# Row maxima 20 steps ahead of the exponentials instead of 22, and a head's row of maxima issued with its last maximum

## The chip, the cores and the metric

The kernel runs on one core of a Trainium2 chip. The metric is the device time of one execution in microseconds (us), lower is better; a time is the median of several runs. Engines are named as the profile names them: PE is the matrix engine (PEld its weight loads), DVE the vector engine, ACT the scalar engine, POOL the GpSimd engine, SP the engine that issues most DMAs.

## What is computed

Two attentions over the same 2048 rows of width 576, 32 heads of width 18 each, are mixed by a gate. A has keys and values per head, B shares one key and one value head among its 32 query heads.

```
x = A_x                                     # 1 x 2048 x 576, float32
g = sigmoid((x * gate_w).sum(-1, keepdims=True))
a = concat_heads(softmax(q_h k_h^T * 18**-0.5) v_h) @ wo       # 32 heads, qkv = x @ A_wqkv
b = concat_heads(softmax(q_h k^T  * 18**-0.5) v) @ wo          # 32 heads, one k and one v
out = g * a + (1 - g) * b
```

All products are made of float32 numbers cut into a high and a low part, so a head's queries and keys take 54 rows (18 times three products) of the 128 partitions, and 54 and 56 rows fit into each half. TensorE can then work on the two halves of its rows at once: rows 64 to 119 for one matmul (`MB`), rows 0 to 55 for another (`SB`).

## The kernel before, in words

The program is one long order written by hand. The 64 heads (0 to 31 of B, 32 to 63 of A) run one after the other. A head has 16 **steps**; step T (0 to 1023, head T // 16) is 128 keys against all 2048 queries: four score matmuls of 512 queries (`step_scores`, L742), four exponentials on ACT (L750), and the products with the values, summed in one PSUM bank `acc` (`step_pv`, L757).

Softmax needs the maximum of each query's scores before its exponentials. So the same scores are also made the other way round, 128 queries against 512 keys at a time, and reduced along the keys (`step_max`, L697). Block M of 128 queries (head M // 16) has 2048 keys, four pieces of 512. A piece is one matmul and one DVE reduction (the letter `m`, L706). Two pieces can also be made by one reduction: ACT takes the relu of the difference of the two (`x`, L700), and DVE adds it to the second piece and reduces (`y`, L703). In the main loop two blocks make one pair: one x, one y, six m. The maxima run `LEAD` steps ahead of the exponentials.

When a head's 16 blocks are reduced, `max_rows` makes the **row of maxima**: DVE reduces the four pieces (L713, tile `m`), transposes (L715, tile `mt`), POOL cuts the result into two parts (L240 and L242, tile `mh`; DVE does it for head 1), SP writes it to DRAM (`m_d`) and, when that has landed, reads it back as two more rows of the head's queries (`qs<-m_d`). The score matmuls of the head multiply these rows by ones, and so the exponent is already reduced by the maximum. The first score matmul of a head therefore waits for the last of these DMAs.

Order around the change:

- The **lead** (`lead_steps`) comes before the main loop. Its string interleaves half matmuls of eight projection units (`A` and `B`, two row halves, L965) with x and y for the first maxima; there every two pieces are one x (L1116) and one y (L1122), so a block has two of each. Two last pieces are plain `m`. The row of head 0 is issued by `lead_max` behind the 32nd y. Eight scores (`s`) end the string: steps 0 and 1.
- The **main loop** takes patterns of 8 steps from T = 2 on: `s` is a score, a digit is that many quarter products with the values, `A`, `B` and `U` are pieces of other projections. `TWO14` (six times from T = 10), `HALF14` (to T = 730), `TWO12` (738 to 802), `HALF12` (802 to 930), `DENSE` (946 to 1002), and `PLAIN` at T = 2, 218, 730, 930 and 938.
- The **tail** is a string of its own, with scores and exponentials only. There the scores of a step alternate between the two row halves (`alone`).
- At each even T `begin(T)` issues the loads that are due and one piece of a slow side job (`slow`: normalising finished heads, on SP, POOL and DVE).
- PSUM has seven banks for all of this. A planner (`Clock`) walks along with a model of the engines and gives each matmul the bank that it expects to be free first. It sets no order.

Before, `max_rows` of a head stood at the start of the pattern in which (T + 22) % 16 = 0, so at T % 16 = 10, six steps before that head's exponentials:

```
        if (T + LEAD) % 16 == 0 and (T + LEAD) // 16 - 1 < NU:
            max_rows((T + LEAD) // 16 - 1, nc.gpsimd if T > 16 else nc.vector)
```

Of the kernel before, what the change touches and what calls it, by code (L numbers as in the profile page):

```python
# [21 lines left out]
NU = 2 * H  # L22
# [2 lines left out]
MT = 14  # L25
ROW_KB, ROW_G, ROW_VB, ROW_Q = 0, 18, 32, 50
SCALE = DH ** -0.5
LEAD = 22
NT = 5
FIRST = ((0, 1), (1, 1), (2, 1), (0, 2), (0, 3), (1, 2), (2, 2), (1, 3), (2, 3))  # L30
PRODS = (("h", "h"), ("h", "l"), ("l", "h"))
# [125 lines left out]
def gated_mix_kernel(ctx: ExitStack, tc: tile.TileContext, xT, wall, wv, wo, out):  # L157
    nc = tc.nc
# [871 lines left out]
    NSTEP = 16 * NU  # L1030
# [31 lines left out]
    slow = [gates()]  # L1062
# [21 lines left out]
                             start=True, stop=True, skip_group_check=True)  # L1084

    pos = {"s": 0, "P": 0, "x": (LEAD + 2) // 2, "y": (LEAD + 2) // 2}
    pairs = {"x": [(M, h) for M0 in range(0, LEAD + 2, 8) for h in range(2) for M in range(M0, M0 + 8)][:-1]}
    pairs["y"] = list(pairs["x"])

    def lead_units():  # L1090
# [36 lines left out]
    def lead_steps(ops):  # L1127

        for op in ops.replace(" ", ""):
# [12 lines left out]
            else:  # L1142
# [5 lines left out]
    lead_steps("AABABABABABxBAABxyABxBAyABxyABxBAyABxyABABxyABABxyABABABxyAB"  # L1148
               "ABxyABABxyABABxyABABxyABABxyABABYBABxBABABxyABABxyABABxyABAB"
               "xyABABxyABABYBABxBAABxyABABxyAgBABxyABABxyABABxyABABYBABxBAA"  # L1150
               "BxyABABxyABABxyABABxyABABxyABABYBABxBAABxyABABxyAgBABxyABABx"
               "yABABxyABABABxyABABxyABABxyAgBABxyABABxyABABxyABAsABxyABABxs"
               "AyABxyABBYsBBBsBB"
               "ssmsms")
    clk.half = HALF_MM

    PLAIN = "mssmsm 4 smsmsm 3 smmssx 3 smmsys 3 mssxysm 3 msxmssm 3 mssysms 3 msssmys 4 msmsms 3 smxssm 3"
# [8 lines left out]
    def begin(T):  # L1166

        for f in at.get(T, []) + at.get(T + 1, []):
            f()
        if slow and T % 16 != 10:  # L1170
            for _ in range(2 if T > 1000 or 914 < T < 930 else 1):
                if slow:
                    try:
                        next(slow[0])
                    except StopIteration:
                        slow.pop(0)

    out_last = out_proj(8, [P])

    def emit(ops, units=0):  # L1180
        for op in ops.replace(" ", ""):
            if op == "s":
                if pos["s"] % 8 == 0:
                    begin(pos["s"] // 4)
                step_scores(*bank(pos["s"]), pos["s"] // 4 >= NSTEP - LEAD, pos["s"] % 4)
                pos["s"] += 1
            elif op == "f":
                keep_busy()
            elif op in "xy":

                if (op == "x" or pos["x"] == pos["y"]) and 2 * pos["x"] < NSTEP:
                    step_max(*divmod(2 * pos["x"], 16), "x")
                    pos["x"] += 1
                if op == "y":
                    step_max(*divmod(2 * pos["y"], 16), 0)
                    pos["y"] += 1
            elif op == "m":
                M, c = plain.pop(0)
                step_max(*divmod(M, 16), c)
            elif op in "AB":  # L1200
                if units:
                    half_step(op.lower())
            elif op == "U":
                u = next_unit() if units else None
                if u:
                    whole_unit(u)
                    units -= 1
            elif op == "V":
                whole_unit(next(out_last))
            elif op in "abc":  # L1210
                if op == "a":
                    while slow:
                        run(slow.pop(0))
                    L["half"] = last_sums(pos["P"] // (4 * NSTEP))
                next(L["half"])
                if op == "a" and not pos["P"] // (4 * NSTEP):
                    next(out_last)
            else:
                n = 1 if op == "P" else int(op)
                while n:  # L1220
                    last, h = divmod(pos["P"], 4 * NSTEP - 64)
                    if last:
                        k = min(n, 2 - h % 2)
                        last_pv(h // 32, h % 32 // 2, 128 * (h % 2), 128 * (h % 2 + k))
                    else:
                        T, a = divmod(pos["P"], 4)
                        k = min(n, 4 - a)
                        step_pv(*divmod(T, 16), 128 * a, 128 * (a + k))
                    pos["P"] += k
                    n -= k  # L1230
                    if pos["P"] % 64 == 0 and pos["P"] < 4 * NSTEP:
                        head_out(pos["P"] // 64 - 1)
# [1 line left out]
    open_ph2()  # L1234
    begin(0)
    emit("x")
    while pos["s"] < 4 * (NSTEP - LEAD):
        T = pos["s"] // 4
        if (T + LEAD) % 16 == 0 and (T + LEAD) // 16 - 1 < NU:
            max_rows((T + LEAD) // 16 - 1, nc.gpsimd if T > 16 else nc.vector)  # L1240
        if T >= SEG[1][3] + 4:
            emit(DENSE, 4)
        elif T in TWICE:
            emit(TWO14, 2)
        elif VB <= T < RB - 8 or RB <= T < RE:
            emit(HALF14, 1)
        elif RE + 8 <= T < RE + 8 * 9:
            emit(TWO12, 2)
        elif RE + 8 * 9 <= T < RE + 8 * 25:
            emit(HALF12, 1)  # L1250
        else:
            emit(PLAIN)
    max_rows(NU - 1)


    emit("ssssss 8 ssssssUssss 7 ssssss 8 ssssss 9 ssssssUssss 7 ssssss 9 ssssssUsssss 7 ssss 6 ssssss 3 a 6 ssssssbUcssss 6 ssssssVVVVVVVVsssssss 9 9 2", 4)
    assert pos["s"] == pos["P"] == 4 * NSTEP
    emit("a V b V V c")
    for u in out_last:
# [35 lines left out]
```

## Time and profile before

| what | value |
|---|---|
| time, median of 3 runs | 2633.17 us (2632.41 to 2634.5) |
| profiled execution: span from first to last instruction | 2632.7 us |
| busy: PE, PEld, DVE, ACT, POOL | 99%, 53%, 91%, 93%, 33% of the span |
| TensorE clock granted | 1.000 |

The page gives the profiled execution as its span alone; no time of its own is shown beside it, and the median of the runs stands 0.4 us above the span. A row of a timeline reads: start and duration in us, engine, line, operation, output<-input, shapes, how many, and in brackets how long the engine sat idle before it and what released it. PE's busy time is modelled to the end of each pipelined matmul, so 99% does not say that it runs at its peak. In the rows, `mx<-bank` is a reduction to maxima, `pt<-bank` an exponential, `bank<-qs,ksb` (L742) a score, `bank<-ksb,qs` (L697) a matmul for a maximum.

### The profile page before, as it was taken

To read this page: it belongs to the slowest core of one execution; us is meant where nothing else is said; L and a number is where in the kernel's file an instruction comes from. 1 tells how busy PE (TensorE), PEld (TensorE's weight loads), DVE (VectorE), ACT (ScalarE), POOL (GpSimd) and SP (SyncE) were. 2 spreads that over 40 slices of the span, in tenths; PEclk is the share of its full clock that TensorE was granted. 3 is DMA by queue.
4 is the path that set the end of the run, shared out by engine and by line. 5 is a ranking of instruction groups with operands and counts; after the bars stand their busy time and mean duration, and the time that the engine had idled before them with its cause. 6 is when DMAs were issued, how large, how long until landed. Compare 5 with 4: busy or idle time off the path is not lost.

```text
span 2632.7 us, 66902 instructions
## 1 busy us (share of the span) xinstructions
PE 2619.6 (99%) x25197; PEld 1402.5 (53%) x25197; DVE 2395.2 (91%) x4575; ACT 2446.7 (93%) x4862; POOL 860.7 (33%) x1108
## 2 busy tenths in 40 slices
PE   9999999999999999999999999999999999999999
PEld 7655545545555455454554555545555544545665
DVE  6899999999999999999999999999998999999883
ACT  5999999999999999999999999999999999999887
POOL 5611000211365535643554446443310020012113
PEclk9999999999999999999999999999999999999999
DMA  8412111212343234323544344434422332233312
GB/s 255 141 58 61 36 48 56 74 52 72 97 117 112 88 98 116 116 90 93 149 133 138 119 130 148 143 116 123 141 95 76 100 97 85 63 88 123 112 56 93
DMA packets 176520, 270.43 MB, mean 103 GB/s; under 512 B 59161, under 2 KB 137705, under 8 KB 164817
## 3 DMA queue, kind: packets, MB, share of 16 engines
q1 hardware_dynamic: 159125, 211.39, 28.1%
q0 software_dynamic: 16032, 53.25, 5.5%
q8 instruction: 198, 3.24, 0.5%
q10 hardware_dynamic: 1040, 1.52, 0.2%
q14 instruction: 125, 1.02, 0.1%
HBM read 190.26 MB, written 66.90 MB: 98 GB/s over the span
## 4 chain that ended last, share of the span: by engine, by line
PE 96%; DMA 1%; POOL 1%; SPq 1%; issue 0%; ACT 0%; DVE 0%; ACTq 0%; POOLq 0%
PE acc L757 39%; PE bank L697 29%; PE bank L742 17%; PE bank L965 10%; SPq L163 1%; PE acc L769 1%; PE bank L945 1%; DMA xsh<-xT 0%; PE bank L278 0%; DMA ksb<-kq 0%; DMA ke<-pdhl 0%; POOL oacc L938 0%; POOL phl L242 0%; POOL pst L1099 0%; POOL qk L163 0%
## 5 line engine op out<-in xcount | busy, mean ns | idle before, releaser
L750 ACT ACTIVATE pt<-bank 128x512 f32<-128x512 f32 x4096 | 2145.0, 616 | 122.8 <-PE bank L742 71.3
L706 DVE TENSOR_REDUCE mx<-bank 128x1 f32<-128x512 f32 x3002 | 1885.7, 683 | 118.6 <-PE bank L742 58.1
L742 PE MATMUL bank<-qs,ksb 56*128 56x512 f32 x2688 | 906.9, 424 | 1.5 <-DMA qs<-m_d 1.5
L697 PE MATMUL bank<-ksb,qs 54*128 54x512 f32 x2270 | 806.4, 426 | 0.0
L757 PE MATMUL acc<-pt,vb 128*19 128x256 f32 (+3 forms) x6144 | 553.1, 455 | 0.0
L697 PEld LDWEIGHTS bank<-ksb,qs 54*128 54x128 f32 x2270 | 382.8, 184 | 319.8 <-ACT pt L750 191.2
L757 PE MATMUL acc<-pt,vg 128*19 128x512 f32 (+3 forms) x5952 | 535.1, 455 | 0.0
L742 PEld LDWEIGHTS bank<-qs,ksb 56*128 56x128 f32 x2688 | 441.0, 184 | 156.2 <-DVE mx L706 63.9
L742 PE MATMUL bank<-qs,ksa 56*128 56x512 f32 x1408 | 466.7, 425 | 0.0
L697 PE MATMUL bank<-ksa,qs 54*128 54x512 f32 x1232 | 438.6, 426 | 0.0
L703 DVE CUSTOM_DVE_ANT_0 junk<-bank,xb 128x512 bf16<-128x512 f32 x500 | 342.5, 685 | 29.6 <-PE bank L742 24.3
L700 ACT ACTIVATE xb<-bank 128x512 f32<-128x512 f32 x500 | 292.3, 606 | 13.8 <-PE bank L742 3.0
L697 PEld LDWEIGHTS bank<-ksa,qs 54*128 54x128 f32 x1232 | 207.8, 184 | 150.5 <-ACT pt L750 86.6
L240 POOL CAST mh<-mt 128x32 fp32r<-128x32 f32 x63 | 13.2, 210 | 827.4 <-DVE mt L715 605.3
L742 PEld LDWEIGHTS bank<-qs,ksa 56*128 56x128 f32 x1408 | 225.5, 184 | 84.2 <-DVE mx L706 31.3
L757 PEld LDWEIGHTS acc<-pt,vb 128*19 128x19 f32 x6144 | 123.1, 97 | 203.0 <-issue 169.5
L757 PEld LDWEIGHTS acc<-pt,vg 128*19 128x19 f32 x5952 | 119.7, 97 | 206.9 <-issue 180.9
L240 POOL CAST rhl<-rst 128x292 fp32r<-128x292 f32 (+2 forms) x81 | 34.0, 420 | 486.4 <-issue 304.7
L965 PE MATMUL bank<-xr,wrh 64*128 64x292 f32 (+1 forms) x1134 | 168.2, 300 | 0.0
L697 PE MATMUL bank<-kdb,qs 54*128 54x512 f32 x372 | 159.8, 429 | 0.0
L965 PEld LDWEIGHTS bank<-xr,wrh 64*128 64x128 f32 x1134 | 139.5, 186 | 2.8
L560 POOL TENSOR_TENSOR xr<-xst,xr 128x876 fp32r<-128x876 f32 (+1 forms) x63 | 130.5, 2071 | 0.0
(173 smaller groups left out, 2403.4 us busy)
## 6 DMA issues: line engine op xcount, KB each, us to landing
qs<-qk SPq DMA_DIRECT2D x366, 144.0 KB
xst<-xT SPq DMA_DIRECT2D x54, 438.0 KB
ksa<-qk SPq DMA_DIRECT2D x132, 144.0 KB
qk<-rhl POOLq DMA_DIRECT2D x54, 292.0 KB, 4.3
ksb<-qk SPq DMA_DIRECT2D x60, 144.0 KB
qk<-phl POOLq DMA_DIRECT2D x16, 512.0 KB, 5.7
onh<-oh POOLq DMA_DIRECT2D x32, 256.0 KB, 4.4
onl<-ol POOLq DMA_DIRECT2D x32, 256.0 KB, 4.8
```

The costliest lines, as they stand in the source:

```text
L163: return (eng or nc.sync).dma_start(o, i)
L240: eng_h.tensor_copy(h, src)
L560: nc.gpsimd.tensor_tensor(x[:, 5:8, 0:n], t0, x[:, 0:3, 0:n].bitcast(F32), op=OP.subtract)
L697: nc.tensor.matmul(pm, qs[u % 3][b:b + 54, i * P:(i + 1) * P], k, start=True, stop=True)
L700: nc.scalar.activation(MX["x", u, i], pm, AF.Relu)
L703: nc.vector.tensor_tensor_reduce(junk, pm, MX.pop(("x", u, i)), 1.0, -3e38, op0=OP.add, op1=OP.max, accum_out=MX[u][:, i, c:c + 1])
L706: nc.vector.tensor_reduce(MX[u][:, i, c:c + 1], pm, axis=AX.X, op=OP.max)
L742: nc.tensor.matmul(ps, kst(u)[b:b + 56, i * P:(i + 1) * P], qs[u % 3][b:b + 56, c * 512:(c + 1) * 512], start=True, stop=True)
L750: nc.scalar.activation(pt, ps, AF.Exp, scale=SCALE)
L757: nc.tensor.matmul(acc[32 * j:32 * j + 19, a:b], v_of(u, i), PT[u, i, j][:, a:b], start=(i == 0), stop=(i == 15), skip_group_check=True)
L769: nc.tensor.matmul(acc[32 * j:32 * j + 19, 256 * half + a:256 * half + b], v_of(NU - 1, i), pt[:, x + a:x + b], start=(i == 0), stop=(i == ...
L965: nc.tensor.matmul(u.fp[op][:, 0:u.n], x[b:b + 64], y[b:b + 64], start=(n == 0), stop=(n == last))
```

## The change

`LEAD` goes from 22 to 20. The lead forms 22 blocks of maxima instead of 24: four times `xy` (eight matmuls) are taken out of its string, one of them ahead of the row of head 0, three behind it, and nothing else in it moves. The main loop begins two blocks earlier in the list of maxima, so the tail loses two steps without maxima and gets one more pair in its place (six m and one y; its x stands in the loop). The rows of maxima are no longer issued at a pattern's start but by `formed`, right behind the seventh reduction of a head's last pair; where that is depends on the pattern's string: 1.75 steps into `HALF14`, 2.25 into `TWO14`, 2 into `TWO12`, 2.75 into `PLAIN`, 3 into `HALF12` and `DENSE`. The side job now pauses at T % 16 = 12 and runs at 10.

```diff
-LEAD = 22
+LEAD = 20
...
-    pairs = {"x": [(M, h) for M0 in range(0, LEAD + 2, 8) for h in range(2) for M in range(M0, M0 + 8)][:-1]}
+    pairs = {"x": [(M, h) for M0 in range(0, LEAD + 2, 8) for h in range(2) for M in range(M0, min(M0 + 8, LEAD + 2))][:-1]}
...
-        if slow and T % 16 != 10:
+        if slow and T % 16 != 12:
...
+    FORMED = {}
+
+    def formed(p):
+
+        FORMED[p] = FORMED.get(p, 0) + 1
+        if FORMED[p] == 7 and p % 8 == 7:
+            max_rows(p // 8, nc.gpsimd if p > 15 else nc.vector)
...
                 if op == "y":
                     step_max(*divmod(2 * pos["y"], 16), 0)
                     pos["y"] += 1
+                    formed(pos["y"] - 1)
             elif op == "m":
                 M, c = plain.pop(0)
                 step_max(*divmod(M, 16), c)
+                formed(M // 2)
...
-    while pos["s"] < 4 * (NSTEP - LEAD):
+    while pos["s"] < 4 * (NSTEP - LEAD - 2):
         T = pos["s"] // 4
-        if (T + LEAD) % 16 == 0 and (T + LEAD) // 16 - 1 < NU:
-            max_rows((T + LEAD) // 16 - 1, nc.gpsimd if T > 16 else nc.vector)
...
-    max_rows(NU - 1)
...
-    emit("ssssss 8 ssssssUssss 7 ssssss 8 ...", 4)
+    emit("msmssm 4 smsmsmsys 4")
+    emit("ssssssUss 7 ssssss 8 ...", 4)
```

In the lead the change is seen on DVE around the row of head 0 (`m_610`, `mt`). A row `L1122 ISA junk,mx<-bank,xd` is a y; `L477` is a piece of the side job. Before:

```order
L1122 ISA junk_1060,mx_600<-bank_1058,xd 128x512
L1122 ISA mx_600 128x1
L1122 ISA junk_1072,mx_600<-bank_1070,xd 128x512
L1122 ISA mx_600 128x1
L1122 ISA junk_1080,mx_600<-bank_1078,xd 128x512
L1122 ISA mx_600 128x1
L713 TENSOR_REDUCE m_610<-mx_600 128x16
L715 STREAM_TRANSPOSE mt<-m_610 128x32
L1122 ISA junk_1108,mx_601<-bank_1106,xd 128x512
```

and now, at the same place:

```order
L1122 ISA junk_1064,mx_600<-bank_1062,xd 128x512
L1122 ISA mx_600 128x1
L1122 ISA junk_1072,mx_600<-bank_1070,xd 128x512
L1122 ISA mx_600 128x1
L1122 ISA junk_1091,mx_600<-bank_1089,xd 128x512
L1122 ISA mx_600 128x1
L713 TENSOR_REDUCE m_610<-mx_600 128x16
L715 STREAM_TRANSPOSE mt<-m_610 128x32
L1122 ISA junk_1112,mx_601<-bank_1110,xd 128x512
```

The row stands behind the same 32nd y. What moved is that y itself: with one `xy` gone ahead of it, it stands eight places later in the string (place 219 counted from 0, not 211), and the piece of the side job follows one y behind the row, not two. On POOL the four rows around the row of head 0 stand as they did, the DMA of a projection unit directly ahead of it, before and now alike:

```order
L242 TENSOR_TENSOR phl<-pst,phl 128x512
L163 DMA qk<-phl 128x2x512
L240 CAST mh<-mt 128x32
L242 TENSOR_TENSOR mh<-mt,mh 128x32
L1099 TENSOR_TENSOR pst<-pst,pst_1031 128x512
```

Nothing moved there. In a `HALF14` pattern, head 13, DVE before: `mx_603` holds head 13's maxima, `mx_604` head 14's, and `L703 ISA junk,mx<-bank,xb` is a y.

```order
L706 TENSOR_REDUCE mx_603<-bank_9793 128x1
L713 TENSOR_REDUCE m_611<-mx_603 128x16
L715 STREAM_TRANSPOSE mt<-m_611 128x32
L703 ISA junk,mx_604<-bank_9809,xb 128x512
L703 ISA mx_604 128x1
L706 TENSOR_REDUCE mx_604<-bank_9817 128x1
L706 TENSOR_REDUCE mx_604<-bank_9828 128x1
L706 TENSOR_REDUCE mx_604<-bank_9835 128x1
L706 TENSOR_REDUCE mx_604<-bank_9846 128x1
L706 TENSOR_REDUCE mx_604<-bank_9853 128x1
L706 TENSOR_REDUCE mx_604<-bank_9864 128x1
L706 TENSOR_REDUCE mx_604<-bank_9871 128x1
```

and now:

```order
L703 ISA junk,mx_603<-bank_9768,xb 128x512
L703 ISA mx_603 128x1
L706 TENSOR_REDUCE mx_603<-bank_9776 128x1
L706 TENSOR_REDUCE mx_603<-bank_9787 128x1
L706 TENSOR_REDUCE mx_603<-bank_9794 128x1
L706 TENSOR_REDUCE mx_603<-bank_9805 128x1
L706 TENSOR_REDUCE mx_603<-bank_9812 128x1
L706 TENSOR_REDUCE mx_603<-bank_9823 128x1
L713 TENSOR_REDUCE m_611<-mx_603 128x16
L715 STREAM_TRANSPOSE mt<-m_611 128x32
L706 TENSOR_REDUCE mx_604<-bank_9839 128x1
L706 TENSOR_REDUCE mx_604<-bank_9846 128x1
```

The two rows L713 and L715 have moved from ahead of the pattern's first y to behind that y and six reductions. At the beginning of the tail, DVE before (L940 adds a projection into the output, L781 is the copy of `acc` at the end of a head):

```order
L706 TENSOR_REDUCE mx_602<-bank_44542 128x1
L706 TENSOR_REDUCE mx_602<-bank_44559 128x1
L940 TENSOR_TENSOR oacc<-bank_44509,oacc 128x288
L713 TENSOR_REDUCE m_611<-mx_602 128x16
L715 STREAM_TRANSPOSE mt<-m_611 128x32
L940 TENSOR_TENSOR oacc<-bank_44640,oacc 128x288
L781 COPY oe<-acc 128x512
```

and now:

```order
L940 TENSOR_TENSOR oacc<-bank_44477,oacc 128x288
L706 TENSOR_REDUCE mx_602<-bank_44545 128x1
L706 TENSOR_REDUCE mx_602<-bank_44552 128x1
L706 TENSOR_REDUCE mx_602<-bank_44563 128x1
L706 TENSOR_REDUCE mx_602<-bank_44574 128x1
L706 TENSOR_REDUCE mx_602<-bank_44581 128x1
L706 TENSOR_REDUCE mx_602<-bank_44588 128x1
L703 ISA junk,mx_602<-bank_44595,xb 128x512
L703 ISA mx_602 128x1
L713 TENSOR_REDUCE m_611<-mx_602 128x16
L715 STREAM_TRANSPOSE mt<-m_611 128x32
L940 TENSOR_TENSOR oacc<-bank_44642,oacc 128x288
```

Seven reductions, those of the last pair, have moved from the lead's side of the list into the tail, ahead of the row of head 63.

More of the change, by code (lines that the diff above doesn't have):

```diff
@@ L1150, in gated_mix_kernel @@
                "xyABABxyABABYBABxBAABxyABABxyAgBABxyABABxyABABxyABABYBABxBAA"
[L1151 to L1154, printed above, removed]
+               "BxyABABxyABABxyABABABABxyABABYBABxBAABxyABABxyAgBABABABxyABA"
+               "BxyABABABABABxyABABxyAgBABABABxyABABxyABAsABxyABABxsAyABxyAB"
+               "BYsBBBsBBssmsms")
     clk.half = HALF_MM
@@ L1252, in gated_mix_kernel @@
             emit(PLAIN)
-    max_rows(NU - 1)
-    emit("ssssss 8 ssssssUssss 7 ssssss 8 ssssss 9 ssssssUssss 7 ssssss 9 ssssssUsssss 7 ssss 6 ssssss 3 a 6 ssssssbUcssss 6 ssssssVVVVVVVVsssssss 9 9 2", 4)
+    emit("msmssm 4 smsmsmsys 4")
+    emit("ssssssUss 7 ssssss 8 ssssss 9 ssssssUssss 7 ssssss 9 ssssssUsssss 7 ssss 6 ssssss 3 a 6 ssssssbUcssss 6 ssssssVVVVVVVVsssssss 9 9 2", 4)
     assert pos["s"] == pos["P"] == 4 * NSTEP
```

## The prediction

> **What bounds the kernel now.** I read the page's busy shares first, then the rate of the exponentials stage by stage, then the timeline around the first exponential, around a row of maxima, and at the start of the tail.
>
> ```profile
> span 2632.7 us, 66902 instructions
> PE 2619.6 (99%) x25197; PEld 1402.5 (53%) x25197; DVE 2395.2 (91%) x4575; ACT 2446.7 (93%) x4862; POOL 860.7 (33%) x1108
> ```
>
> PE, DVE and ACT are all above 90%, so no share says which of them sets the pace. The table of stretches, restricted to the exponentials (L750), gives the pace: busy time, count, clock.
>
> ```profile
> 627.90:646.70 18.80, 16.69 (x33) 1.00 0.37 101
> 2116.00:2300.00 184.00, 159.33 (x306) 1.00 0.28 84
> 2441.00:2556.00 115.00, 86.45 (x160) 1.00 0.28 85
> 2567.00:2586.00 19.00, 19.00 (x39) 1.00 0.07 16
> ```
>
> One exponential takes 0.570 us in `PLAIN` (18.80/33), 0.601 in `HALF12`, 0.719 in `DENSE`, and 0.487 in the tail, where ACT is busy without a gap. So ACT sets the pace only in the tail. In the main loop it is the common order of PE, DVE and ACT with seven banks between them. Which engine waits there is seen in one `HALF14` pattern (590 to 609 us, the waits):
>
> ```profile
> PEld bank L697 <- ACT pt L750: 2.7, 4, 0.8
> PEld bank L697 <- DVE mx L706: 0.8, 2, 0.4
> ```
>
> PE waits for banks of ACT more than for banks of DVE, and part of these waits lies under matmuls that still run.
>
> **The lead: four xy removed.** Stretches with all engines (PE, PEld, DVE, ACT, POOL), and then the rows around the row of head 0:
>
> ```profile
> 80.00:85.00 5.00, 5.00 (x44) 3.94 (x42) 4.68 (x16) 4.51 (x9) 4.47 (x7) 1.00 0.53 184
> 85.00:90.00 5.00, 3.53 (x31) 2.62 (x29) 2.79 (x9) 3.46 (x8) 4.38 (x5) 1.00 0.33 111
> ...
> 79.24 0.22 DVE L713 TENSOR_REDUCE m<-mx 128x16 f32<-128x64 f32 x1
> 79.49 0.21 DVE L715 STREAM_TRANSPOSE mt<-m 128x32 f32<-128x32 f32 x1
> ...
> 81.04 0.73 POOL L163 DMA_DIRECT2D qk<-phl  x1 [0.30 <-POOL phl L242]
> 81.77 0.22 POOL L240 CAST mh<-mt 128x32 fp32r<-128x32 f32 x1
> ...
> 82.35 0.34 SPq L163 DMA_DIRECT2D m_d<-mh  x1
> 85.27 1.25 SPq L163 DMA_DIRECT2D qs<-m_d  x2
> ...
> 88.73 0.49 PE L742 MATMUL bank<-qs,ksb 56*128 56x512 f32 x1 [1.47 <-DMA qs<-m_d]
> 89.26 0.60 ACT L750 ACTIVATE pt<-bank 128x512 f32<-128x512 f32 x1 [1.54 <-PE bank L742]
> ```
>
> Until 85 us PE issues 44 matmuls in 5 us, so eight matmuls less are 0.91 us of PE's time; that is what the shorter string is worth at most while PE paces. But the string doesn't set when the exponentials begin. PE reached the first score 1.47 us before its rows of maxima had landed. Follow the chain back: the read was issued at 85.27 because the write `m_d` had to land first, the write stood behind POOL's `mh` at 81.77, and POOL took `mh` only then because it was still busy with a projection unit: its DMA issue of 81.04 ends at 81.77 with no gap, 2.07 us after DVE had `mt` (79.70). That unit's last B stands ahead of the first xy removed, and the order of POOL is unchanged. The 32nd y now comes eight places later in the string, 8 x 5/44 = 0.91 us, so `mt` is there at about 80.6, still 1.2 us before POOL asks for it. Hence `mh`, the write, the read and the first score stay at 81.77, 82.35, 85.27 and 88.73; PE is at the first score 0.91 us earlier and idles 2.4 us instead of 1.47. Behind the first score nothing is removed. I take 0 for the lead. Ends: SP waited for 64 writes of `m_d` 87.6 us in all, 1.37 each,
>
> ```profile
> SPq L163 <- DMA m_d<-mh: 87.6, 64, 2.8
> ```
>
> and this one took 2.58 (82.69 to 85.27), so the chain may be 1.2 us shorter by luck; longer than 2.8 none was. So -1.2 to +0.2. The four relu and four y that go with the eight matmuls are covered by the same idle time.
>
> **The main loop: the row of maxima later in a pattern.** Two questions: does it disturb DVE at its new place, and does it still land in time. DVE in the half of `HALF14` with the row, then in the half without (there the copy of `acc` stands at the same place):
>
> ```profile
> 589.12 0.22 DVE L713 TENSOR_REDUCE m<-mx 128x16 f32<-128x64 f32 x1
> 589.77 0.69 DVE L703 CUSTOM_DVE_ANT_0 junk<-bank,xb 128x512 bf16<-128x512 f32 x1
> 590.39 6.08 DVE L706 TENSOR_REDUCE mx<-bank 128x1 f32<-128x512 f32 x10
> 596.85 0.69 DVE L706 TENSOR_REDUCE mx<-bank 128x1 f32<-128x512 f32 x1 [0.39 <-PE bank L742]
> ...
> 609.29 0.68 DVE L703 CUSTOM_DVE_ANT_0 junk<-bank,xb 128x512 bf16<-128x512 f32 x1
> 609.89 6.06 DVE L706 TENSOR_REDUCE mx<-bank 128x1 f32<-128x512 f32 x10
> 616.27 0.69 DVE L706 TENSOR_REDUCE mx<-bank 128x1 f32<-128x512 f32 x1 [0.31 <-PE bank L742]
> ```
>
> The row costs DVE 0.65 us (589.12 to 589.77). Then come ten reductions without a gap, then 0.39 us in which DVE waits for PE: there the delay has been absorbed. In the changed `HALF14` (heads 4 to 13 and 15 to 45, 41 in all) the row stands behind the sixth of these reductions, so still ahead of that idle time: the end of the run stays where it is. 0. Ends: the two halves run 19.52 us (589.77 to 609.29) and, from head to head at 38.83, 19.31; half of that difference, 0.1 us a head, is 4 us either way. In `HALF12` (heads 51 to 58) the row comes later, behind one idle time of DVE and ahead of others:
>
> ```profile
> 2115.22 0.22 DVE L713 TENSOR_REDUCE m<-mx 128x16 f32<-128x64 f32 x1
> 2121.11 1.29 DVE L706 TENSOR_REDUCE mx<-bank 128x1 f32<-128x512 f32 x2 [0.25 <-PE bank L742]
> 2122.92 0.08 DVE L703 DVE_READ_ACCUMULATOR2_ANT mx<- 128x1 f32 x1
> 2126.78 4.96 DVE L706 TENSOR_REDUCE mx<-bank 128x1 f32<-128x512 f32 x8 [0.25 <-PE bank L742]
> 2133.30 0.69 DVE L706 TENSOR_REDUCE mx<-bank 128x1 f32<-128x512 f32 x1 [0.35 <-PE bank L742]
> ...
> 2116.39 0.36 SPq L163 DMA_DIRECT2D m_d<-mh  x1
> 2117.87 1.24 SPq L163 DMA_DIRECT2D qs<-m_d  x2
> ...
> 2129.58 0.50 PE L742 MATMUL bank<-qs,ksb 56*128 56x512 f32 x1
> ```
>
> It will stand behind 2122.92; the two idle times that follow, 0.25 and 0.35, take 0.60 of its 0.65. Until then DVE gives back banks up to 0.4 us later: 0 to 0.4 us for each of eight heads, 0 to 3; the bank waits above are mostly ACT's, so I take 0.
>
> In time: from the row's start to the end of the second read's issue it is 3.89 us (2115.22 to 2119.11). The landing is bounded by a head whose row was late, head 31: POOL had been held up, and
>
> ```profile
> 1297.60 0.22 POOL L240 CAST mh<-mt 128x32 fp32r<-128x32 f32 x1
> 1300.39 1.25 SPq L163 DMA_DIRECT2D qs<-m_d  x2
> 1303.39 0.39 PE L742 MATMUL bank<-qs,ksb 56*128 56x512 f32 x1
> ```
>
> its first score stood at 1303.39 without a wait, so reads land within 1.75 us of the end of their issue. A round trip is at most 5.64 us. In `HALF12`, the shortest lead with `DENSE` at three steps, the changed row starts at 2123.00 of this time scale and the score stands at 2129.58: 6.58 us, 0.94 to spare. `HALF14` has 1.25 steps more, `DENSE` longer steps. In head 31 POOL's delay lasts past the new start of the row (about 1293.5), so its `mh` stays at 1297.60 and its score in time. No head waits: 0.
>
> The Trainium skill weighs against this: "DMA: Bandwidth & Descriptors", section "Anatomy of one DMA", puts a fixed cost of about 2.0 us on each DMA, nearly all of it the receipt of the write (for DMAs that GpSimd issues). With two of them in a row the round trip would be an estimated 1.17 + 2.0 + 1.24 + 2.0 = 6.4 us, and the spare time 0.2 instead of 0.9. By that rule too no head waits, but little would be needed. The write above was waited for 1.48 us from issue to issue, so this trace is below the rule.
>
> **The tail: two steps get maxima.** Steps 1002 and 1003 had scores alone, 8 x 0.487 = 3.90 us. Now they carry six m and one y. By the `PLAIN` rate they take 8 x 0.570 = 4.56; by `DENSE` 5.75, but no projection is among them; DVE alone needs 7 x 0.606 = 4.24 (6.06 for ten). I take `PLAIN`, +0.7, with ends +0.3 and +1.9. One x more in the last `DENSE` pattern hides, ACT being busy 86.45 of 115 there. The row of head 63 follows:
>
> ```profile
> 2566.38 0.21 DVE L713 TENSOR_REDUCE m<-mx 128x16 f32<-128x64 f32 x1
> 2569.74 2.51 SPq L163 DMA_DIRECT2D qs<-m_d  x4
> 2576.92 1.03 PE L742 MATMUL bank<-qs,ksa 56*128 56x512 f32 x6
> ```
>
> It begins seven reductions later, 2570.6, has two of its four reads issued 4.61 us after that and all four after 5.87, and needs up to 1.75 more: 2577.0 and 2578.2. The head's first score stood at about 2577.2 and moves with the 0.7 to 2577.9, the second, from the other half, right behind. Just in time; 0 to 0.5 us of waiting, I take 0.1.
>
> **Sum:** 0 + 0 + 0.7 + 0.1 = +0.8 us on the span of 2632.7, so 2633.5; the median of the runs stands 0.4 above that span, 2634.0.
>
> **Rivals.** (1) Rows too late, slower. Place: heads 51 to 58, from a round trip over 6.58 us; each microsecond beyond costs eight. A write of 2.8 us, the longest, instead of 1.48 gives 6.96 and 3 us in all. The side job now runs at T % 16 = 10 ahead of `mh` on POOL; with its cast, subtraction and wait in the way another 0.5 us or more is thinkable, some 0.9 us a head, 2641. For: the spare time is short. Against: that job starts three steps before the row. (2) Relief in the main loop, faster: with 0.65 us gone from ahead of the run of ten, PE gets its first banks sooner, and 0.2 us in each of 41 heads stay: -8, 2625. For: DVE runs without a gap there. Against: PE waits for ACT more. (3) The 0.91 us of the lead do arrive, because the write of `m_d` lands sooner: 2633.1. Against: nothing ahead of it on POOL or in the queue has changed.
>
> **How the numbers follow.** My forecast has 0.70 and by its terms' ends 2631.5 to 2638; rival 1 has 0.10, rival 2 0.08, rival 3 0.12. A change below 0.2% (5.3 us) can hardly be told from none here. Rival 3 and nearly all of the forecast lie within that: same 0.79. Faster 0.09 is rival 2 and a bit; slower 0.12 is rival 1 and the upper ends of tail and main loop together. The range 2630.0 to 2638.5 leaves out rivals 1 and 2 for the most part.
>
> **What would show it.** The first exponential again near 89.3 us, with PE's wait for `qs<-m_d` at some 2.4 us; no other wait of PE for that DMA over 0.3 us; head to head 38.8 us in `HALF14`; about 0.8 us more from step 1002 to 1008. Wrong it would be if the first exponential came sooner by more than 1 us, if heads 51 to 58 showed that wait, or if a head in `HALF14` took another time by 0.1 us.

## The result, and the profile after

The changed kernel takes 2668.37 us (median of four runs, 2667.68 to 2672.01); the kernel before took 2633.84 us beside it (2632.41 to 2634.69). The ratio is 1.0131, 95% interval 1.0119 to 1.0143: slower by 34.5 us, where 2634.0 was forecast. The profiled execution has a span of 2665.7 us, 33.0 more than before. First the page of the changed kernel, span and busy times: DVE, ACT and POOL are busy within 6 us of what they were before, so the 33 us are waiting, or PE at work for longer.

```profile
span 2665.7 us, 66816 instructions
PE 2642.5 (99%) x25197; PEld 1407.1 (53%) x25197; DVE 2393.8 (90%) x4575; ACT 2452.2 (92%) x4859; POOL 861.4 (32%) x1108
```

Where the 33 us lie is read from the starts of the exponentials (L750), four to a step. "Block u" below is the time from head u's first exponential to head u+1's; it holds the row of maxima of head u+1. Each figure is a block's length less the same block's in the kernel before, in us, from the profiled executions.

| blocks | what is in them | changed kernel |
|---|---|---|
| start | up to the first exponential | +0.78 |
| 0 | | +1.91 |
| 1, 2 | `TWO14` | +0.61 |
| 3 to 12, 15 to 44 | `HALF14`, 40 blocks | +12.57 (median +0.30) |
| 13, 14 | row of head 14 in `PLAIN` | +9.13 |
| 45 to 49 | `TWO12` mostly | +1.18 |
| 50 to 56 | `HALF12` | +3.12 |
| 57 | the normalising of tile 7 | +1.76 |
| 58 to 61 | `DENSE` | +0.34 |
| 62 | start of the tail | +1.67 |
| 63 to the end | | -0.12 |

**The lead.** The same rows as were shown of before, on POOL, SP's queue, PE and ACT, and then stretches of 3.41 us (busy time and count of PE, PEld, DVE, ACT, POOL; then the granted clock, the DMAs' share and GB/s):

```profile
80.04 0.22 DVE L713 TENSOR_REDUCE m<-mx 128x16 f32<-128x64 f32 x1
81.86 0.22 POOL L240 CAST mh<-mt 128x32 fp32r<-128x32 f32 x1
82.45 0.34 SPq L163 DMA_DIRECT2D m_d<-mh  x1
85.67 1.25 SPq L163 DMA_DIRECT2D qs<-m_d  x2
89.53 0.46 PE L742 MATMUL bank<-qs,ksb 56*128 56x512 f32 x1 [3.42 <-DMA qs<-m_d]
90.03 0.60 ACT L750 ACTIVATE pt<-bank 128x512 f32<-128x512 f32 x1 [3.65 <-PE bank L742]
```

```profile
87.06:90.47 3.41, 0.94 (x8) 0.92 (x10) 0.00 (x0) 0.43 (x1) 2.97 (x4) 1.00 0.50 163
90.47:93.88 3.41, 3.41 (x18) 2.83 (x15) 2.10 (x6) 2.82 (x6) 0.62 (x1) 0.50 0.41 154
```

POOL takes `mh` 0.09 us later than before, as forecast. But the write took 3.22 us from issue to the read's issue (before 2.92), and the score followed 3.86 us behind the read's issue (before 3.46), so PE idled 3.42 us, and behind that its clock was 0.50 for one stretch of 3.41 us. In the kernel before it was 1.00 until the last 2.5 us. (The start differs between the profiles of all these kernels: the reduction of head 0's row stands between 78.5 us, in c2, and 82.5 us, in e5. So the +0.78 of the table's first row is no more than profiles differ by; the differences between rows of one profile are what counts here.)

**The main loop.** DVE at the row of head 13, the same place as was shown of before:

```profile
596.22 0.69 DVE L703 CUSTOM_DVE_ANT_0 junk<-bank,xb 128x512 bf16<-128x512 f32 x1 [0.67 <-PE bank L742]
596.84 3.67 DVE L706 TENSOR_REDUCE mx<-bank 128x1 f32<-128x512 f32 x6
600.54 0.22 DVE L713 TENSOR_REDUCE m<-mx 128x16 f32<-128x64 f32 x1
601.00 2.44 DVE L706 TENSOR_REDUCE mx<-bank 128x1 f32<-128x512 f32 x4
603.66 2.48 DVE L706 TENSOR_REDUCE mx<-bank 128x1 f32<-128x512 f32 x4 [0.21 <-PE bank L742]
```

The 0.65 us that the row took ahead of the run are not gone: DVE now waits 0.67 us for PE there. The row had stood in a wait. In the run it stands between reductions that PE's banks hang on, and PE has a new wait, seen in the waits (total, times, longest); the other two lines are those of the row's DMA (four waits, 3.42 us at head 0, 5.82 at head 14, 0.29 at head 53 and 0.57 at head 54) and of the sums:

```profile
PEld bank L697 <- DVE m L713: 14.8, 35, 0.4
PE bank L742 <- DMA qs<-m_d: 10.1, 4, 5.8
DVE sm L821 <- DMA sm<-sum_d: 4.8, 2, 3.5
```

**Head 14.** DVE, POOL, SP's queue and PE, and the stretches behind:

```profile
642.50 0.22 DVE L713 TENSOR_REDUCE m<-mx 128x16 f32<-128x64 f32 x1
646.59 1.56 POOL L242 TENSOR_TENSOR wrl<-wrst,wrh 128x640 fp32r<-128x640 f32 x1
648.10 0.20 POOL L240 CAST mh<-mt 128x32 fp32r<-128x32 f32 x1
648.18 1.48 SPq L163 DMA_DIRECT2D wrst<-wall  x3
649.76 0.53 SPq L163 DMA_DIRECT2D m_d<-mh  x1
651.75 1.24 SPq L163 DMA_DIRECT2D qs<-m_d  x2
654.51 0.76 PE L742 MATMUL bank<-qs,ksb 56*128 56x512 f32 x1 [5.82 <-DMA qs<-m_d]
```

```profile
648.00:656.00 8.00, 2.19 (x15) 0.95 (x15) 1.84 (x4) 2.31 (x6) 5.57 (x8) 0.64 0.27 75
656.00:660.00 4.00, 4.00 (x34) 1.60 (x30) 2.31 (x6) 2.03 (x4) 0.00 (x0) 0.50 0.52 164
```

`mh` comes 5.6 us behind the row's reduction: at step 218 the second projection starts (`row_units`), and since the row is issued inside the pattern now, it stands behind that start's work on POOL (`xr`, `wrh`, `wrl`) and its loads on SP's queue (`wrst`). Before, it stood ahead of them.

**The tail.** ACT at steps 1002 to 1007, before (the run of 28 begins with step 1002), and then now, from the third exponential of step 1005 on:

```profile
2567.00 13.83 ACT L750 ACTIVATE pt<-bank 128x512 f32<-128x512 f32 x28 [0.42 <-PE bank L742]
```

```profile
2606.72 2.61 ACT L750 ACTIVATE pt<-bank 128x512 f32<-128x512 f32 x5 [0.66 <-PE acc L757]
```

Steps 1002 and 1003, which carry the new pair of maxima, take 0.41 and 0.33 us more than before. Step 1005, which carries none, takes 0.85 more: ACT sits idle for 0.66 us in it, released by a product with the values, where it ran without a gap before. PE does not wait for the row of head 63.

### The profile page after: what moved, and what is told of

Read it like the earlier page. It is cut to its first block, busy times and chain, and to the rows that moved or that the text cites. A ratio compares the mean times of both kernels' runs of the same rounds, so it can differ in the third digit from the quotient of the medians.

```text
span 2665.7 us, 66816 instructions
## 1 busy us (share of the span) xinstructions
PE 2642.5 (99%) x25197; PEld 1407.1 (53%) x25197; DVE 2393.8 (90%) x4575; ACT 2452.2 (92%) x4859; POOL 861.4 (32%) x1108
## 3 DMA queue, kind: packets, MB, share of 16 engines
q14 instruction: 124, 1.02, 0.1%
## 4 chain that ended last, share of the span: by engine, by line
PE 93%; DMA 2%; POOL 1%; SPq 1%; DVE 1%; issue 1%; ACT 0%; ACTq 0%; POOLq 0%; DVEq 0%
PE acc L757 37%; PE bank L697 28%; PE bank L742 17%; PE bank L965 10%; SPq L163 1%; DVE mx L706 1%; PE acc L769 1%; PE bank L945 1%; DMA m_d<-mh 0%; DMA qs<-m_d 0%; DMA xsh<-xT 0%; POOL phl L242 0%; POOL pst L1099 0%; DMA ksa<-qk 0%; PE bank L278 0%
## 5 line engine op out<-in xcount | busy, mean ns | idle before, releaser
L750 ACT ACTIVATE pt<-bank 128x512 f32<-128x512 f32 x4096 | 2151.2, 615 | 149.8 <-PE bank L742 89.1
L697 PE MATMUL bank<-ksb,qs 54*128 54x512 f32 x2277 | 819.6, 428 | 1.2 <-DVE mx L706 1.1
L703 DVE CUSTOM_DVE_ANT_0 junk<-bank,xb 128x512 bf16<-128x512 f32 x501 | 343.6, 686 | 51.4 <-PE bank L742 44.8
```

What stands on the lines that cost most here:

```text
L697: nc.tensor.matmul(pm, qs[u % 3][b:b + 54, i * P:(i + 1) * P], k, start=True, stop=True)
L703: nc.vector.tensor_tensor_reduce(junk, pm, MX.pop(("x", u, i)), 1.0, -3e38, op0=OP.add, op1=OP.max, accum_out=MX[u][:, i, c:c + 1])
L750: nc.scalar.activation(pt, ps, AF.Exp, scale=SCALE)
```

## The experiments

Beside each time stands its ratio to the kernel before, run on the same chip; its runs there had medians between 2633.68 and 2636.02 us. Blocks are compared as in the table above.

### e1_rows_late: the rows' new place alone

Kernel before, lead of 22:

```diff
-        if (T + LEAD) % 16 == 0 and (T + LEAD) // 16 - 1 < NU:
-            max_rows((T + LEAD) // 16 - 1, nc.gpsimd if T > 16 else nc.vector)
+    def formed(p):      # called behind every reduction, as in the change; the side job's pause moves too
+        FORMED[p] = FORMED.get(p, 0) + 1
+        if FORMED[p] == 7 and p % 8 == 0 and p > 12:
+            max_rows(p // 8 - 1, nc.gpsimd if p > 16 else nc.vector)
```

> The kernel before with its lead of 22 blocks; only the rows of maxima are issued as late as in the changed kernel (behind the seventh reduction of the next head's first pair), and the side job pauses at T % 16 = 12. Theory A, the rows' new place is what costs: 0.3 us a head from head 4 to 58 (about 17 us), 8.5 to 9 us at head 14, where the row falls behind the start of the second projection, and about 2 us at heads 53, 54 and 58: about 2661 us. Theory B, what costs is the maxima formed only 20 steps ahead (the shorter lead, fewer blocks in stock): 2634 to 2636 us here.

2658.62 us, ratio 1.0085 (1.0070 to 1.0100), so some 22 of the 34 us. Theory B falls, theory A holds: `HALF14` +9.63 (median +0.20), blocks 13 and 14 +7.51, block 57 +1.28. Expected were 27 us over the kernel before, measured 22: in `HALF14` a block loses less than in the changed kernel. The start with block 0 costs 0.56 here instead of 2.69, the tail nothing. DVE at the row of head 13:

```profile
593.24 0.69 DVE L703 CUSTOM_DVE_ANT_0 junk<-bank,xb 128x512 bf16<-128x512 f32 x1 [0.73 <-PE bank L697]
593.86 3.67 DVE L706 TENSOR_REDUCE mx<-bank 128x1 f32<-128x512 f32 x6
597.45 0.21 DVE L713 TENSOR_REDUCE m<-mx 128x16 f32<-128x64 f32 x1
597.90 2.44 DVE L706 TENSOR_REDUCE mx<-bank 128x1 f32<-128x512 f32 x4
```

The wait ahead of the run is about the same. But the row starts 3.59 us behind the run's start (593.86 to 597.45), in the changed kernel 3.70 (596.84 to 600.54): there it reads the maximum that the reduction directly ahead has just written, here maxima that have long been there.

### e2_split_late: DVE's part at the pattern's start, the rest later in the order

```diff
-            max_rows((T + LEAD) // 16 - 1, nc.gpsimd if T > 16 else nc.vector)
+            max_rows((T + LEAD) // 16 - 1, nc.gpsimd if T > 16 else nc.vector, True)
...
+        if FORMED[p] == 7 and p % 8 == 0 and p > 12:
+            LATE.pop(p // 8 - 1)()    # mh, the write, the reads
```

> As e1_rows_late, but the two operations of a row on DVE (reduction and transpose) stay at the pattern's start; only POOL's mh, the write and the reads come late. Theory A1, the 0.3 us a head is DVE's: the operations used to stand where DVE waits for PE at the pattern's start, and now delay reductions: HALF14 heads as in the kernel before (38.83 us each), and only head 14 (8.5 to 9 us) and heads 53, 54 and 58 (2 us) remain: about 2644 us. Theory A2, it is POOL's or the queue's later place: about 2661 us, as e1_rows_late.

2641.63 us, ratio 1.0023 (1.0013 to 1.0032). `HALF14` is back to the kernel before (median +0.02), and blocks 13 and 14 keep +6.20. Blocks 52, 53 and 57, of which I expected 2 us, lose 0.20, 0.00 and 0.00. The pause of the side job is moved here as in e1 and in the changed kernel, so that move isn't what costs `HALF14` its time. The reason limits what the run says of theory A2: POOL and the queue are free at that time and run ahead, so `mh` of head 13 came at 588.51, 0.60 us behind the reduction at 587.91. Written later, it was not done later, except where other work stood in between, at head 14. So here the later order on POOL and SP cost time where something is queued between, at head 14. A2 is left to e8.

### e3_prelude_later: the second projection starts behind the row

```diff
-    when(RB - 8, lambda: (early("px"), begin_units(row_units())))
+    when(RB - 4, lambda: (early("px"), begin_units(row_units())))
```

> The changed kernel, with the start of the second projection (cutting x, splitting weights, loads) put four steps later, at step 222 instead of 218, so behind the row of head 14. If head 14 lost its 9 us because POOL and the queue had that work ahead of the row: PE's wait of 5.8 us for the row and the half clock behind it go, 2668.4 - 8.5 = 2660 us (2659 to 2661). Rival: the row in PLAIN comes too late by itself (2.75 steps into the pattern), then PE still waits there and the time stays above 2665 us; the later start could also make the first units late, by up to 2 us.

2660.62 us, ratio 1.0097 (1.0082 to 1.0112), against 1.0131: 9 us less. Blocks 13 and 14 lose 0.44 instead of 9.13, and the clock stays full there. `HALF14` is at +14.37 instead of +12.57, but that is not the later start of the projection: e4 and e9, which leave it where it was, are at +14.94 and +13.83. Part of the difference lies at head 31, whose first score waits for its row in these three profiles (0.49, 0.87 and 0.77 us) and not in the changed kernel's. POOL at the row of head 14, and the stretches behind:

```profile
642.42 0.21 POOL L240 CAST mh<-mt 128x32 fp32r<-128x32 f32 x1 [41.43 <-DVE mt L715]
```

```profile
648.00:656.00 8.00, 8.00 (x81) 3.66 (x84) 7.69 (x15) 7.70 (x17) 2.44 (x3) 1.00 0.82 222
656.00:660.00 4.00, 4.00 (x52) 1.88 (x44) 4.00 (x8) 3.79 (x9) 3.78 (x5) 1.00 0.02 4
```

### e4_lead_dve: the row of head 0 without POOL

```diff
-            max_rows(0)
+            max_rows(0, nc.vector)
```

> The changed kernel, with mh of head 0 (cast and subtraction) on DVE instead of POOL. Theory: the start is set by the row of head 0, which waited for POOL; without that wait the write of m_d is issued about 1.3 us sooner (at 81.1 instead of 82.45), PE idles about 2.1 us instead of 3.42, the granted clock stays at 1.00 behind it, and the first exponential comes at 88.7 instead of 90.03; with the half clock gone (2 us over the first 16 steps) 2668.4 - 3.3 = 2665 us. Rival: the half clock has nothing to do with the length of PE's wait: 2667 us, with the clock at 0.5 behind the wait as before. Second rival: other work bounds the start, first exponential near 90.0 and 2668 us.

2664.91 us, ratio 1.0110 (1.0095 to 1.0125), 5.5 us less than the changed kernel, though the two intervals overlap; in the profiles start and block 0 together are 4.3 us less. SP's queue, PE and ACT:

```profile
81.08 0.34 SPq L163 DMA_DIRECT2D m_d<-mh  x1
83.75 1.26 SPq L163 DMA_DIRECT2D qs<-m_d  x2
86.53 0.46 PE L742 MATMUL bank<-qs,ksb 56*128 56x512 f32 x1
87.03 0.60 ACT L750 ACTIVATE pt<-bank 128x512 f32<-128x512 f32 x1
```

The write went out at 81.08 as expected, and the rest went faster too (2.67 us to the read's issue, and at most 2.78 from there to the landing, where the changed kernel had 3.22 and 3.86). PE doesn't wait at all, the clock stays at 1.00, the first exponential comes 3.0 us sooner, and block 0 loses 0.58 instead of 1.91. Both rivals fall. So 1.3 us of block 0 go with the wait and the half clock, the rest is not theirs. The other kernels with 20 steps agree: where one stretch of half clock follows the wait, block 0 loses 1.64 to 1.91 us (the changed kernel, e3, e5, e7, e9), with two stretches 2.27 (e6), with none 0.45 to 0.58 (e4, c1, c2).

### e5_lead_fill: PE kept busy ahead of the first score

```diff
-               "BxyABABABABABxyABABxyAgBABABABxyABABxyABAsABxyABABxsAyABxyAB"
+               "BxyABABABABABxyABABxyAgBABABABxyABABxyABAffffsABxyABABxsAyABxyAB"
```

> The changed kernel with eight matmuls without use (four times 512 and 256 columns, into acc, which is free then) ahead of the first score, so that PE isn't idle for 3.4 us there; the row of head 0 is not sooner. Theory: the granted clock goes to 0.5 because PE was idle that long, and not because the score was late: PE's wait is 1 to 2 us, the clock stays at 1.00 from 88 to 96 us, and from the first exponential to step 16 it takes 1.9 us less than in the changed kernel, about as long as before (within 0.3 us). Rival: the clock falls all the same, or the lateness of the score costs the 1.9 us by itself: step 16 as late as in the changed kernel.

2666.63 us in its one run. Inconclusive on what it was made for, and a surprise: the eight matmuls took 1.5 us only, PE still waited 2.20 us, less than the 3.41 us that I thought were needed, and the clock fell all the same. Block 0 lost 1.76. PE, and two stretches:

```profile
88.40 1.26 PE L1083 MATMUL acc<-ident_r 56*128 56x256 f32 x7
91.86 0.60 PE L742 MATMUL bank<-qs,ksb 56*128 56x512 f32 x1 [2.20 <-DMA qs<-m_d]
```

```profile
88.64:92.05 3.41, 1.21 (x9) 0.88 (x9) 0.48 (x2) 0.24 (x1) 3.24 (x4) 1.00 0.48 163
92.05:95.46 3.41, 3.41 (x18) 3.12 (x18) 1.00 (x3) 2.17 (x4) 1.25 (x2) 0.50 0.39 150
```

So the forecast's own figure, 2.4 us of idle time, could have been long enough to halve the clock. Whether the clock or the wait costs block 0 its time no run separates: in e4 both are gone. That the loss doesn't grow with the wait (1.76 us here behind 2.20, 1.64 in e7 behind 3.23) speaks for the clock.

### e6_one_later and e7_four_later: other places for the row

```diff
         FORMED[p] = FORMED.get(p, 0) + 1
-        if FORMED[p] == 7 and p % 8 == 7:
-            max_rows(p // 8, nc.gpsimd if p > 15 else nc.vector)
+        if FORMED[p] == 7 and p % 8 == 7:
+            HELD[:] = [p, n]      # e6: n = 1 up to step 800; e7: n = 4 in HALF14; else 0
+        elif HELD:
+            HELD[1] -= 1
+        if HELD and HELD[1] == 0: ...    # shortened: max_rows, and HELD is emptied
```

> The changed kernel, with each row of maxima up to step 800 one reduction later. The row in the changed kernel directly follows the reduction that writes its last maximum, and starts 0.12 us later than the next reduction would have; in e1_rows_late, where the maxima had long been there, a HALF14 head lost 0.17 us and not 0.30. Theory D, DVE waits for its own last result: one reduction between them takes 0.12 us from each of some 46 heads: 2668.4 - 5.5 = 2663 us, HALF14 heads at +0.17. Rival: what differs from e1_rows_late is something else (the two steps less): heads still at +0.30, 2668 us.

> The changed kernel, with the rows in HALF14 (41 heads) four reductions later, behind the run of ten, where DVE then waits about 0.2 to 0.4 us for PE. Theory E, a row costs what of its 0.45 to 0.65 us doesn't fit into an idle time of DVE that is there anyway: behind the run it costs 0.0 to 0.1 us a head instead of 0.30: 2668.4 - 0.25 x 41 = 2658 us. Rival F, any place other than the pattern's start costs the same 0.3 us: 2668 us.

e6: 2657.35 us, ratio 1.0089 (1.0074 to 1.0104), 11 us less than the changed kernel, twice what was expected: `HALF14` +4.87, median +0.08 and not +0.17. e7: 2657.58 us, ratio 1.0084 (1.0067 to 1.0101), 12 us less: `HALF14` +3.60, median +0.02. Theory E holds, F falls; of D the direction holds, the size doesn't. DVE in e6, then in e7:

```profile
595.66 4.27 DVE L706 TENSOR_REDUCE mx<-bank 128x1 f32<-128x512 f32 x7
599.85 0.20 DVE L713 TENSOR_REDUCE m<-mx 128x16 f32<-128x64 f32 x1
600.29 4.32 DVE L706 TENSOR_REDUCE mx<-bank 128x1 f32<-128x512 f32 x7
```

```profile
595.35 6.09 DVE L706 TENSOR_REDUCE mx<-bank 128x1 f32<-128x512 f32 x10
601.36 0.21 DVE L713 TENSOR_REDUCE m<-mx 128x16 f32<-128x64 f32 x1
```

In e6 the row starts 4.19 us behind the run's start, seven times 0.598: the 0.11 us of waiting for its own last result are gone. The row takes 0.44 us there. DVE then runs on without the idle time of 0.21 us that e1 and the changed kernel still have, so that more of the row is absorbed than one reduction earlier. In e7 the row lies in that idle time altogether. Not all of the 40 blocks are at the median in either kernel: a few (30, 31, 37, 38) lose 0.4 us or more in one profile and not in the next; and the first score of head 30, 31 or 38 then waits for its row's DMA (in e6 0.68 us at head 31, in e7 0.57, 0.39 and 0.76 at the three). At head 31 b1 has such a wait too, 0.32 us, with its rows at the old place. Whether these waits account for the whole loss stays open.

### e8_extra_row: a second row that only DVE knows

Kernel before, called at e1's place:

```diff
+    def extra_row(u):
+        nc.vector.tensor_reduce(dm[:, 0:16], mxs[u] if u < 2 else mxs[2 + u % 3], axis=AX.X, op=OP.max, negate=True)
+        nc.vector.transpose(dt, dm)
```

> The kernel before, its rows where they were; in addition, at the changed kernel's place, a second reduction 128x64 and a transpose of the same size into tiles that nobody reads (62 heads), of which neither POOL, nor a DMA, nor the planner of the banks knows. Theory A1, it is DVE's time at that place: the same 0.17 us a HALF14 head as in e1_rows_late and 0.2 to 0.3 in the others, no loss at heads 14, 53, 54 and 58: about 10 us over the kernel before, 2644 us. Theory A2, the loss comes from POOL's and the queue's later work or from the planner's banks: within 2 us of the kernel before.

2645.80 us, ratio 1.0044 (1.0029 to 1.0059): 12 us, theory A1. `HALF14` +7.62, median +0.17; blocks 13 and 14 +0.32. A2 falls: no POOL, no DMA and no planner is needed for the loss in `HALF14`. In `HALF12` the extra row costs 0.09 a block (median), the changed kernel's 0.34, e1's 0.21. The 0.13 between the last two would fit the wait for the last maximum; what e1 has above e8 there stays open. Block 57 loses 0.62 here, from DVE's time alone.

### e9_sums_first: block 57

```diff
-        if u == NU - 2:
+        if u in (56, NU - 2):
             sums()
...
-        if u < NU - 2:
+        if u < NU - 2 and u != 56:
             sums()
```

> The changed kernel; only in head 56 the DMA of the row sums is issued ahead of the eight pieces of the output instead of behind them. Theory G, head 57 loses 1.4 to 1.8 us because the later row of maxima keeps the loads behind it on SP's queue, so that the sums come late and DVE's reciprocal at step 919 waits for them with reductions queued behind it: with the sums 5 us sooner DVE doesn't wait there, and from head 57's first exponential to head 58's it takes 0.3 us more than before instead of 1.76. Rival: the loss there is the row's place itself; still 1.4 us or more. As a whole 2667 us; one run can't tell that from 2668.

2666.44 us in one run. Block 57 loses 0.90 instead of 1.76: a part of theory G. (With the sums in their old place it loses 1.31 to 2.22 in e3 to e7, and c2, which has this edit too, again 0.96.) The reciprocal on DVE, which had no such wait before, in the changed kernel and then in e9:

```profile
2369.77 0.95 DVE L821 RECIPROCAL sm<-sm 112x128 f32<-112x128 f32 x1 [1.30 <-DMA sm<-sum_d]
```

```profile
2368.43 0.95 DVE L821 RECIPROCAL sm<-sm 112x128 f32<-112x128 f32 x1 [0.46 <-DMA sm<-sum_d]
```

The wait shrank from 1.30 to 0.46 us, not to nothing: the sums went out first, but their read stands on the same queue behind the eight pieces of the output.

### b1_lead_dve: e4's edit in the kernel before

> The kernel before (22 blocks, rows at the pattern's start), with only mh of head 0 on DVE instead of POOL. Theory: as in e4_lead_dve the write of m_d is issued at about 81.1 instead of 82.35, PE no longer waits for the row (1.47 us idle before), and the first exponential comes 1.4 us sooner, at about 87.9; nothing else changes: 2633.8 - 1.4 = 2632.4 us, ratio 0.9995. Rival: the two operations on DVE delay the lead's maxima by their 0.5 us, and what PE no longer waits for it loses there: 2633.3 to 2634.3 us.

2635.59 us, ratio 1.0002 (0.9993 to 1.0011): no difference. PE no longer waits for the row, but the first exponential comes only 0.74 us sooner, and block 0 is 0.74 longer: what PE no longer waits comes back within 16 steps. Rival and theory lie within the interval together; by the blocks of this one profile it looks like the rival. One loss is seen on DVE and POOL:

```profile
79.11 1.29 POOL L242 TENSOR_TENSOR phl<-pst,phl 128x512 fp32r<-128x512 f32 x1
79.43 1.02 DVE L240 CAST mh<-mt 128x32 fp32r<-128x32 f32 x1
```

### c1_after_mended and c2_more_mended: do the parts add up?

c1 is the changed kernel with the edits of e3, e4 and e7; c2 adds e9's and the rows of `TWO14`, `PLAIN` and `TWO12` one reduction later.

> The changed kernel with three edits at once: mh of head 0 on DVE (e4_lead_dve), the second projection begun at step 222 (e3_prelude_later), the rows in HALF14 four reductions later (e7_four_later). Theory: the costs have separate places and add up: 2668.4 - 4.3 (lead) - 8.7 (head 14) - 10.5 (HALF14) = 2645 us; what is left over the kernel before is 0.2 to 0.35 us a head in the other patterns (some 5 us), heads 53, 54 and 58 (some 3 us), and the tail (1.6 us), less what the lead gains. Rival: time won at one place is lost at the next, 2650 us or more.

> c1_after_mended with two more edits: the sums of head 56 first (e9_sums_first), and the rows in TWO14, PLAIN and TWO12 one reduction later. Theory: each takes away its own part, 1.5 to 3 us at head 57 and 0.12 to 0.2 us in some 8 heads (1 to 1.5 us): 2648.4 - 3.5 = 2645 us. What is left over the kernel before, the tail (1.6 us), HALF12 (0.3 us a head) and the waits of heads 52 and 53, can't be had at these places. Rival: no part of head 57's loss goes: 2647 us or more.

c1: 2648.39 us, ratio 1.0048 (1.0034 to 1.0062), 22 us of the 34.5 gone. Expected were 23.4. `HALF14` is at +2.63 (median +0.01), blocks 13 and 14 at +0.89, start and block 0 at -1.71 together (-2.28 and +0.57); block 57 got worse, +3.29, with a stretch of half clock. c2: 2644.41 us, ratio 1.0038 (1.0024 to 1.0052); block 57 is at +0.96 and has no half clock, the start is 1.6 us sooner, no more than profiles differ by, and the other parts are much as in c1. The parts have separate places. What is left is the tail (block 62, +1.64), `HALF12` (+2.88), block 57 and some 5 us in small pieces, less 3.4 at the start and block 0. No version with 20 steps came back to the kernel before.

## Why the prediction was wrong, point by point

**Lead, taken as 0.** Right: POOL and the queue set the row of head 0, the first exponential came no sooner, PE arrived earlier (by 1.15 us, 86.11 instead of 87.26) and idled. The step that failed: "idles 2.4 us instead of 1.47" was costed at nothing. The upper end of 0.2 was too low too, since write and reads landed 0.8 us later. Behind 3.42 us of idle time the clock was halved; wait and half clock cost block 0 1.3 us of its 1.91 (e4), and with the 0.78 of the start, which may be chance, the two lost 2.7. The Trainium skill, "TensorE: Matmul & The Clock Gate", section "Part 1: The HAM clock gate (the "warmup" mystery)", has the rule that I left out: the clock falls to half after an idle window of about 3.4 us, and the windows are free-running, 3413 ns each. The trace agrees on the length, 3.41 us; but a wait of 2.20 us was enough here, in a stretch in which PE was busy for 1.21 us (e5).

**Main loop, taken as 0.** The step that failed is "there the delay has been absorbed ... the end of the run stays where it is". From two halves of a pattern with the same timing, one with the row and one with the copy of `acc`, I read what the row costs; but both have something of about that size in the same place, so neither showed what DVE does without it. It waits: 0.67 us for PE. The row had cost nothing, and any place inside the run costs what doesn't fit into the idle time behind (e7: 0.02 a block, e6: 0.08, e1 and e8: about 0.2). In the changed kernel 0.11 us come on top, because the row directly follows the reduction that writes its last maximum. I gave ends of 4 us either way; it was 12.57 us in 40 blocks, and in other profiles with the rows at the same place up to 14.94 (e4).

**In time, taken as 0.** "No head waits" failed at one place for a reason that I should have seen: in the changed order POOL's `wrh` and `wrl` stand ahead of `mh` of head 14, and I worked out the round trip for other patterns and passed over `PLAIN`. It cost 9.13 us, a wait of 5.82 us and 10.24 us at half clock (650.26 to 660.50), which is three times 3.41; with the same order the loss was 6.08 us in e5, with one such stretch. e3 shows it. Elsewhere the bound of 5.64 us was too low, since it took a write at 1.48 us: at head 54 the write took 3.36 us from its issue to the read's issue, and the score waited 0.57 us. The kernel before showed that spread already: the median of its 64 writes is 1.49 us from issue to issue, and the longest 3.18. The 2.8 of the prediction is the same spread counted from the end of the write's issue, so rival 1, which put it in the place of 1.48, was priced too low.

```profile
2229.30 0.35 SPq L163 DMA_DIRECT2D m_d<-mh  x1
2232.66 1.25 SPq L163 DMA_DIRECT2D qs<-m_d  x2
2235.65 0.47 PE L742 MATMUL bank<-qs,ksa 56*128 56x512 f32 x1 [0.57 <-DMA qs<-m_d]
```

By the fixed cost of 2.0 us, which the prediction quoted from the Trainium skill ("DMA: Bandwidth & Descriptors", section "Anatomy of one DMA") and set against a row below it, the spare time was an estimated 0.2 us; this write, at 3.36 us, is above that figure.

**`HALF12`, 0 to 3 us, taken as 0.** It was 3.12 in the seven blocks 50 to 56, just over the upper end; the forecast counted eight heads, and with block 57 it is 4.88.

**Block 57, not in the prediction.** I had asked who waits behind the row on DVE and POOL, and not who stands behind it on SP's queue. Part of its 1.76 us goes that way (e9), and part is DVE's time (e8).

**Tail, +0.7 and 0.1.** 1.67 in block 62, within the ends of +0.3 and +1.9, but in part by luck. The two steps with maxima took 0.74 us more, as the `PLAIN` rate had said. The row of head 63 was not waited for. The other 0.85 us, in step 1005, was not in the prediction: ACT waits there for a product. The tail's new string has the projection piece `U` behind 14 scores and not 12, and two scores between it and the next products where there were four; whether that or the new matmuls for maxima make the product late, no run tests.

**The sum.** 0 + 0 + 0.7 + 0.1, in the order lead, main loop with rows in time, tail and its row, against 2.7 (lead), 12.6 (`HALF14`), 9.1 (head 14) and 1.7 (tail), and 6.9 in what was not or hardly costed (the other blocks of the table, 0.61 + 1.18 + 3.12 + 1.76 + 0.34 - 0.12). The prediction's "2631.5 to 2638" is also not what its terms' ends add up to: from 2633.1 they reach from 2628.2 (-1.2, -4, +0.3) to 2642.7 (+0.2, +4, +3, +1.9, +0.5), and that doesn't hold 2668 either.

**The rivals:** the first, rows too late, did happen, with less than 1 us at heads 53 and 54, and at head 14, where I had not placed it. The second, relief from the 0.65 us ahead of the run, had the wrong sign. The third didn't come about with POOL in the chain; past POOL, in e4, c1 and c2, start and block 0 together are at -1.65, -1.71 and -3.42; since the start differs by as much between profiles, it isn't shown that this is the shorter lead.

## What to carry to other kernels

An operation that seems to cost its full length may stand in a wait: look for what its engine would do without it before counting its removal as a gain, and count its new place in full unless an idle time behind it takes it. Follow a moved step through each queue it goes through, at every place where it now falls behind something else; the one exceptional place (here one head of 64) can cost more than a third of the rest together. Idle time of the matrix unit is not free: here waits of 2.2 us and more halved its clock for the next 3.4 us or longer.

## What was not expected of the hardware

The changes of the clock lie on a fixed grid of 3.41 us: in the changed kernel it fell at 90.47 and at 650.26, and rose at 93.89, 163 times 3.413 us earlier than the second fall. At the first score the clock stayed after waits of 1.47, 1.51 and 1.54 us (the kernel before, e1, e8) and fell after 2.20 (e5), 2.83 (e9), 3.10 (e3), 3.23 (e7), 3.42 and 3.45 us (e6). In c1 it fell after a stretch in which PE waited for 0.99 us at most and was busy for longer:

```profile
2346.32:2349.73 3.41, 2.42 (x18) 0.96 (x14) 2.60 (x5) 2.29 (x5) 0.45 (x1) 1.00 0.17 49
2349.73:2353.14 3.41, 3.41 (x21) 1.17 (x18) 2.94 (x5) 1.57 (x3) 0.00 (x0) 0.50 0.40 97
```

In the kernel before, whose one change of clock at 2630.25 puts a line of the grid at 87.32, the stretch from there to 90.73 had PE busy for 2.00 us and was not caught. So the busy time that the trace shows isn't what decides alone; what does, stays open.

A cast of 128x32 on DVE took longer where POOL was at work. In the changed kernel the cast of head 1's row, with no instruction on POOL beside it, took DVE 0.18 us, and in the kernel before, beside a subtraction on POOL, 0.48. In b1 that of head 0 took 1.02 us and ended 0.05 us behind a subtraction on POOL (79.11 + 1.29 = 80.40, 79.43 + 1.02 = 80.45), and in c1 0.37 us, again at the end of one:

```profile
79.30 1.30 POOL L242 TENSOR_TENSOR phl<-pst,phl 128x512 fp32r<-128x512 f32 x1
80.26 0.37 DVE L240 CAST mh<-mt 128x32 fp32r<-128x32 f32 x1
```

"SBUF — State Buffer" of the Trainium skill, section "Terms", says that DVE and GpSimd take one pair of ports by turns, the whole instruction long. These rows agree; no run here was made to test it.
